# Moving set-up work and the first block's transfers to other engines in a planned recurrence and feed-forward kernel

## The chip, the cores and the metric

The kernel runs on one core of a Trainium2 chip. The metric is the device time of one execution in microseconds; the median of several executions is compared. A profile of one execution gives the rows quoted below; in them PE is TensorE, PEld its weight loads, DVE is VectorE, ACT is ScalarE, POOL is GpSimd and SP is the engine that mostly issues transfers. A name with q (SPq, ACTq) is the engine's own queue of issues and waits.

## What is computed

The reference has three parts, one feeding the next. The first is a recurrence over 768 time steps for 4 x 8 heads of width 40:

```python
for t in range(S):
    y[:, :, t] = einsum('bhd,bhde->bhe', rt, state)
    Sa = einsum('bhde,bhe->bhd', state, at)
    state = state * wt[:, :, None, :] - einsum('bhd,bhe->bhde', Sa, bt)
    state = state + einsum('bhd,bhe->bhde', vt, kt)
...
h = x @ w_in;  x = (h * tanh(softplus(h))) @ w_out
h = x @ w_in2; out = (h * cos(h)) @ w_out2
```

The two feed-forward layers take 3072 tokens of width 320 through 2048 hidden units, in float32, each matmul split into high and low parts that run as fp32r.

## The kernel before

The recurrence is cut into 24 chunks of 32 time steps, and the 32 heads into two halves of 16, so there are 48 steps g = 0 to 47 (chunk c = g // 2, half hf = g % 2). For each step a function pre prepares what does not depend on the state: a load IN, two scans on VectorE (L584, L592), two products AM (L600), a product KB (L606), 32 matmuls (L630), and a masked product (L643) that is stored to DRAM as l_d (L663, L664). For a batch of steps (the first batch has four steps, 0 to 3, the others two) inverse loads l_d back as XM in another layout (L707), runs 28 small steps (L722, L724; on VectorE for the first two batches, on GpSimd from the third), stores t_d (L735) and loads it as TT (L741). halves (L770 to L773) completes the inverse with the masks lowd and lowm, which setup_tf makes (L372 to L380). Then chain runs the part that depends on the state: stages of matmuls rhs (L837), zmm (L851), ztm (L860, L883), rvz (L909), f (L935) and stm (L985), with evictions by ScalarE and VectorE between them. Two steps of a chunk are mates: a stage of one can be held back until the other's is ready, so that both run without a change of TensorE's tile shape.

Every two chunks give the outputs of 256 tokens, a block. yst stores Y of each half to x_d in DRAM (L1004, L1005), and layer1 loads the block back as XR (L1098 to L1100), splits it into XH (L1107) and XL (L1109), runs the first layer's matmuls h_tasks (L1045) and outs (L1026), with Mish on ScalarE (L1123, L1125) and the difference GL on VectorE (L1128). There are 12 such blocks. The second layer (L1060, L1077) follows at the end.

The weights come as pairs of 32-bit words. prep loads each piece (L468), converts it with ScalarE (L475) and two or three VectorE steps (L480, L485), copies the high part (L402 or L404) and has GpSimd subtract it (L515). Its list of pieces, jobs, has 25 for the first layer, 12 of w_in and 13 of w_out. The raw words have three buffers.

All of this is put into the engines' instruction streams by a planner, Plan. Each task has an engine (or a choice), an estimated duration, predecessors, buffers that it takes from rings, and a priority prio where a lower number goes first. run simulates the engines and always takes the task that can begin earliest, then by rank (for TensorE, by tile shape and mates) and prio. The order that results is the order in each engine's stream, and an engine works through its stream strictly in order; the waits in the program follow from the data alone. So predecessors that only the planner knows shape the order and are no waits. The priorities around the change: pre(g) has -5000 + 10g, inverse -5000 + 10(g0 + cnt) - 32, chain(g) -10000 + 10g, the weight words of the first layer -4921, and the first block's input load -9955.

These lines set what the change touches: the order of the weight loads (in prep),

```python
preds=(after if layer == 2 else [tt_ld[2]] if len(loads) >= W1_FREE else [t_in[2]]) + ([t_sw] if late else [])
    + (loads[-AHEAD_W:][:1] * (len(loads) >= AHEAD_W) if len(loads) >= W1_FREE else loads[-1:]),
```

and the short conversion (Prelu with a slope that keeps the sign), which is taken where `two` holds:

```python
two = layer == 1 and not late
```

## Time and profile before

| what | us |
|---|---|
| median of three executions | 1088.33 |
| their lowest and highest | 1087.53, 1093.37 |
| the profiled execution, its own time | 1083.14 |
| its span, first to last instruction | 1081.0 |
| TensorE busy in the span | 1016.0 (94%) |
| VectorE, ScalarE, GpSimd busy | 728.4, 545.7, 419.6 |

The span is what the rows are measured in; the execution's own time holds some 2 us around it. A row of an engine's order of time gives start, duration, engine, line, operation, result and operands with their shapes, how many were merged into the row, and in brackets the idle time of the engine before it with what ended it.

### The profile page before, as it was taken

What the parts mean: (1) busy time and instruction counts of PE and PEld (TensorE: products, weight loads), DVE (VectorE), ACT (ScalarE), POOL (GpSimd) and SP (SyncE); (2) the same over time, 40 slices, a digit from 0 to 9 for tenths busy, and PEclk for the clock granted to TensorE, in tenths of its full rate; (3) what the DMA queues carried; (4) which work ended last, traced back from release to release, by engine and by line L of the source; (5) the groups of instructions that cost most, each with busy time, mean ns of one, the idle gap of its engine ahead of it and who ended that gap; (6) DMA issues with size and microseconds to landing.
All of it is one profiled execution on the core that took longest, in us unless ns stands there. A gap on an engine that the chain in (4) does not pass through costs nothing.

```text
span 1081.0 us, 36651 instructions
## 1 busy us (share of the span) xinstructions
PE 1016.0 (94%) x15112; PEld 934.8 (86%) x15112; DVE 728.4 (67%) x1542; ACT 545.7 (50%) x1338; POOL 419.6 (39%) x862
## 2 busy tenths in 40 slices
PE   3289898999999999999999999999999999999998
PEld 3177787888888988989989999999999999999997
DVE  8598977767857678577653798545555656565555
ACT  1166676664656556566475454444433434353433
POOL 3124665353554627546530144103333333333332
PEclk9999799999999999999999999999999999999999
DMA  4567745646545555456452454211100202010100
GB/s 109 152 196 227 216 130 158 174 114 172 148 124 158 132 151 157 127 136 167 118 144 63 156 164 125 87 47 30 43 13 1 55 1 54 1 40 1 25 1 25
DMA packets 109014, 111.90 MB, mean 104 GB/s; under 512 B 64048, under 2 KB 88624, under 8 KB 108848
## 3 DMA queue, kind: packets, MB, share of 16 engines
q1 hardware_dynamic: 103952, 108.19, 36.2%
q8 instruction: 119, 1.95, 0.8%
q10 hardware_dynamic: 4896, 1.38, 0.6%
q14 instruction: 47, 0.39, 0.1%
HBM read 91.43 MB, written 18.09 MB: 101 GB/s over the span
## 4 chain that ended last, share of the span: by engine, by line
PE 47%; DVE 2%; issue 1%; ACT 0%; DVEq 0%
PE bank L1060 14%; PE bank L1077 13%; PE bank L1045 9%; PE bank L1026 9%; PE bank L1172 1%; PE bank L935 1%; DVE GL L1128 0%; PE bank L883 0%; DVE AU L485 0%; PE bank L837 0%; ACT GH L1125 0%; PE bank L851 0%; PE bank L909 0%; DVE AU L493 0%; DVE FR L919 0%
## 5 line engine op out<-in xcount | busy, mean ns | idle before, releaser
L1211 POOL TENSOR_TENSOR GL<-H,GH 128x512 fp32r<-128x512 f32 x94 | 122.0, 1298 | 239.2 <-ACT GH L1209 223.6
L724 POOL TENSOR_TENSOR XT<-XM 64x14 f32<-64x14 f32 (+6 forms) x294 | 98.4, 335 | 162.9 <-DMA XM<-l_d 129.3
L402 ACT ACTIVATE FL<-bank 64x160 f32<-64x160 f32 (+1 forms) x376 | 101.8, 296 | 117.4 <-PE bank L674 62.5
L1202 ACT ACTIVATE T<-T,half_pi 128x512 f32<-128x512 f32 x96 | 69.4, 723 | 104.3 <-DVE T L1199 104.3
L1128 DVE TENSOR_TENSOR GL<-H,GH 128x512 fp32r<-128x512 f32 x96 | 70.3, 736 | 71.9 <-ACT GH L1125 64.0
L1195 DVE TENSOR_SCALAR T<-bank 128x512 f32<-128x512 f32 x96 | 66.4, 692 | 75.6 <-PE bank L1060 63.4
L722 POOL TENSOR_TENSOR XM<-XM,XT 64x14 f32<-64x14 f32 (+6 forms) x294 | 101.3, 345 | 22.6
L1204 DVE TENSOR_TENSOR H<-bank,T 128x512 f32<-128x512 f32 x96 | 66.1, 689 | 54.4 <-ACT T L1202 53.9
L1123 ACT ACTIVATE H<-bank 128x512 f32<-128x512 f32 x96 | 57.5, 599 | 88.3 <-PE bank L1045 86.1
L1209 ACT ACTIVATE GH<-H 128x512 fp32r<-128x512 f32 x96 | 60.6, 632 | 71.5 <-DVE H L1204 71.5
L1045 PE MATMUL bank<-XH,wih 128*128 128x256 f32 x448 | 94.7, 293 | 0.3 <-ACT XH L1107 0.3
L1045 PE MATMUL bank<-XL,wih 128*128 128x256 f32 x448 | 89.3, 281 | 0.5 <-DVE XL L1109 0.5
L1045 PE MATMUL bank<-XH,wil 128*128 128x256 f32 x448 | 89.3, 281 | 0.0
L1045 PEld LDWEIGHTS bank<-XH,wih 128*128 128x128 f32 x448 | 69.8, 191 | 2.5 <-ACT XH L1107 0.5
L1045 PEld LDWEIGHTS bank<-XL,wih 128*128 128x128 f32 x448 | 69.2, 191 | 0.8 <-DVE XL L1109 0.8
L1045 PEld LDWEIGHTS bank<-XH,wil 128*128 128x128 f32 x448 | 69.1, 191 | 0.0
L1199 DVE SCALAR_TENSOR_TENSOR T<-T,bank 128x512 f32<-128x512 f32 x96 | 65.7, 685 | 2.4
L1045 PE MATMUL bank<-XH,wix 128*128 128x256 f32 x224 | 67.1, 300 | 0.0
L935 PE MATMUL bank<-FR,FL 104*64 104x72 f32 x1536 | 63.2, 240 | 2.4 <-issue 1.1
L1026 PE MATMUL bank<-woh1a,GH 128*128 128x320 f32 x192 | 64.9, 338 | 0.0
L935 PEld LDWEIGHTS bank<-FR,FL 104*64 104x64 f32 x1536 | 56.7, 147 | 7.5 <-DVE FR L919 3.1
L1045 PE MATMUL bank<-XL,wix 128*128 128x256 f32 x224 | 62.9, 281 | 0.0
(189 smaller groups left out, 2859.0 us busy)
## 6 DMA issues: line engine op xcount, KB each, us to landing
VR<-in_vR_dram SPq DMA_DIRECT2D x96, 160.0 KB
IN<-in_inT_dram SPq DMA_DIRECT2D x94, 161.4 KB
FR<-in_rI_dram SPq DMA_DIRECT2D x48, 180.0 KB
FR<-in_vF_dram SPq DMA_DIRECT2D x48, 144.0 KB
RA<-in_w_in_dram SPq DMA_DIRECT2D x12, 512.0 KB
RA<-in_w_out_dram SPq DMA_DIRECT2D x10, 512.0 KB
SV<-in_vS_dram SPq DMA_DIRECT2D x96, 52.0 KB
TMP<-in_w_in_dram SPq DMA_DIRECT2D x8, 512.0 KB
```

The source lines that it names most:

```text
L402: A.activation(o, i, AF.Copy)
L722: IE.tensor_tensor(out=b[:, 0:i, i + 1:16], in0=b[:, 0:i, i + 1:16], in1=tv, op=ALU.add)
L724: IE.tensor_tensor(out=tv, in0=bc(b[:, i:i + 1, i + 1:16], (2 * n, i, w)), in1=bc(b[:, 0:i, i:i + 1], (2 * n, i, w)), op=ALU.mult)
L935: PE.matmul(fp[64 * p:64 * p + 64, qp], fl()[0:104, n * D:n * D + 64], fr()[:, n], start=True, stop=True)
L1026: PE.matmul(o, l[:, f, tsl], r, start=(first and f == 0 and i == 0), stop=(last and f == 1 and i == 2))
L1045: PE.matmul(hp[:, f], pss[i][0], pss[i][1], start=(i == 0), stop=(i == 7))
L1060: PE.matmul(bank[P.at((key, "h"))][:, 0:512], pss[i][0], pss[i][1], start=(i == 0), stop=(i == 7))
L1077: PE.matmul(o, l, r, start=(ft == 0 and i == 0), stop=(ft == NFF - 1 and i == 2))
L1128: gl = P.add(GLE, (dve(512),), lambda eng, Hv=Hv, key=key: EN[eng].tensor_tensor(out=GL_t[P.at((key, "gl"))], in0=Hv(), in1=GH_t[P.at((key ...
L1195: a = P.add("DVE", dve(512), lambda f=f, hv=hv, Tv=Tv: V.tensor_scalar(out=Tv(f), in0=hv(), scalar1=0.25, scalar2=MAGIC, op0=ALU.add, op1= ...
L1202: c = P.add("ACT", act(512, False, 1), lambda f=f, Tv=Tv: A.activation(Tv(f), Tv(f), AF.Sin, scale=-TWO_PI, bias=half_pi), preds=[b], aset ...
L1211: gl = P.add(*((VG, (pool(512), dve(512))) if final and quad == 7 else ("POOL", pool(512))), lambda eng, f=f, Hv=Hv, key=key: EN[eng].tens ...
```

## The change

The diff does eight things. Y's store and the input load of the first block are issued by ScalarE's queue instead of SP's, with an estimated 2.5 us until they land. setup_tf, which makes the masks, runs on GpSimd instead of VectorE. The four clears of SV on VectorE in the first two steps' loads go; setup_v clears these buffers on GpSimd already. The weight loads: the third to the fifth follow the load of XM in the plan (before, the third and fourth followed IN of step 2 and the fifth followed TT's second load), and each of the first five follows the one before it. The weight words' priority goes from -4921 to -4941. Tasks with a priority up to -9890, that is chain and halves of steps 0 to 11, are no longer held back by age or for a mate. The estimate of GpSimd's inverse steps becomes 0.28 us with 0.06 us of latency. The short conversion is limited to the first 30 words.

```diff
--- before.py
+++ after.py
@@ -85,6 +85,7 @@
         "chain.zmm": "32x32", "halves.mm.f": "32x32", "chain.stm": "64x128", "chain.ztm": "full"}
 LEAVE, CHANGE, ENTER = 0.22, 0.12, 0.13
 AGE = 3.0
+EAGER = -1e4 + 110
 WAIT = 8.0
 SP_SAFE = 1.0
 RATE, LAND = 200.0, 1.6
@@ -180,9 +181,9 @@
                             rank = 2.0
                         elif t.mode == last_mode != "full":
                             rank = -1.0
-                        elif t.soft and last_mode == "full" and st - t.ready[e] < AGE:
+                        elif t.soft and t.prio > EAGER and last_mode == "full" and st - t.ready[e] < AGE:
                             rank = 1.5
-                        elif t.mate and last_mode == "full" and st - t.ready[e] < WAIT and t.mate.end is None and (
+                        elif t.mate and t.prio > EAGER and last_mode == "full" and st - t.ready[e] < WAIT and t.mate.end is None and (
                                 t.mate.n_wait or t.mate.ready[e] > st):
                             rank = 1.5
                     key = (max(st - t.pull if e == "DVE" else st, f + SLACK[e]), rank, t.prio + (5e4 if sw else 0), order[id(t)])
@@ -369,15 +370,15 @@
 
     def setup_tf():
 
-        V.memset(lowd, 0.0)
+        G.memset(lowd, 0.0)
         for i in range(4):
             r = slice(32 * i, 32 * i + 32)
-            V.tensor_copy(lowd[r, 16:32], ident[r, 32 * i + 16:32 * i + 32])
+            G.tensor_copy(lowd[r, 16:32], ident[r, 32 * i + 16:32 * i + 32])
         tmp = TB[:, 0]
-        V.tensor_tensor(out=tmp[:, 0:8], in0=lowd[:, 16:24], in1=lowd[:, 24:32], op=ALU.add)
-        V.tensor_tensor(out=tmp[:, 8:12], in0=tmp[:, 0:4], in1=tmp[:, 4:8], op=ALU.add)
-        V.tensor_tensor(out=tmp[:, 12:14], in0=tmp[:, 8:10], in1=tmp[:, 10:12], op=ALU.add)
-        V.tensor_tensor(out=lowm, in0=tmp[:, 12:13], in1=tmp[:, 13:14], op=ALU.add)
+        G.tensor_tensor(out=tmp[:, 0:8], in0=lowd[:, 16:24], in1=lowd[:, 24:32], op=ALU.add)
+        G.tensor_tensor(out=tmp[:, 8:12], in0=tmp[:, 0:4], in1=tmp[:, 4:8], op=ALU.add)
+        G.tensor_tensor(out=tmp[:, 12:14], in0=tmp[:, 8:10], in1=tmp[:, 10:12], op=ALU.add)
+        G.tensor_tensor(out=lowm, in0=tmp[:, 12:13], in1=tmp[:, 13:14], op=ALU.add)
 
     def setup_x():
         G.memset(XM, 0.0)
@@ -423,10 +424,11 @@
     INV_LEAD = 32
     OWN = 2
     SPLIT = 14
-    QUICK = 4
+    QUICK, QUICK_B = 4, 1
     EARLY = 1
+    TWO = 30
     AHEAD_W = 5
-    W1_FREE = 4
+    W1_EARLY, W1_FREE = 2, 5
     DIRECT = 4
     HV_D, HV_P = (0.4, 0.43), 0.52
     B_HI2 = 1.0
@@ -436,7 +438,7 @@
     LOE2, LOD2 = ("POOL", "DVE"), (pool(512), dve(512))
     B_CH, B_HI = 1.3, 0.6
     W1_AFTER = lambda: None
-    W1_G, W1_PRIO = 1, -4921.0
+    W1_G, W1_PRIO = 1, -4941.0
     W2_PRIO = 5e3
     G_POOL = lambda m: m % 2 == 1
 
@@ -466,10 +468,10 @@
                 "p (n w) -> p n w", w=2)
             av = uv = lambda key=key, aring=aring, n=n: STG[aring][P.at((key, "a"))][:, 0:n]
             t0 = P.add("SP", 0.5, lambda raw=raw, src=src: SP.dma_start(raw().rearrange("p n w -> p (n w)"), src),
-                       preds=(after if layer == 2 else [tt_ld[2]] if len(loads) >= W1_FREE else [t_in[2]]) + ([t_sw] if late else []) + (loads[-AHEAD_W:][:1] * (len(loads) >= AHEAD_W) if len(loads) >= W1_FREE else loads[-1:]),
+                       preds=(after if layer == 2 else [tt_ld[2]] if len(loads) >= W1_FREE else [inv_ld[0]] if len(loads) >= W1_EARLY else [t_in[2]]) + ([t_sw] if late else []) + (loads[-AHEAD_W:][:1] * (len(loads) >= AHEAD_W) if len(loads) >= W1_FREE else loads[-1:]),
                        acq=[(rring, (key, "r"))], kb=0.5 * n, prio=prio)
             loads.append(t0)
-            two = layer == 1 and not late
+            two = layer == 1 and not late and len(loads) <= TWO
             f, more = (AF.Prelu, {"alpha": NEGATIVE}) if two else (AF.Copy, {})
             t1 = P.add("ACT", act(n, False),
                        lambda raw=raw, av=av, f=f, more=more: A.activation(
@@ -727,7 +729,7 @@
 
         for i in range(1, 15):
             for add in range(2):
-                t = P.add("POOL" if own else "DVE", 0.1 + 0.0022 * i * (15 - i) if own else 0.165, step(i, add), preds=[t], lat=0.1 if own else 0.04, prio=pr, port=True)
+                t = P.add("POOL" if own else "DVE", 0.28 if own else 0.165, step(i, add), preds=[t], lat=0.06 if own else 0.04, prio=pr, port=True)
         t = P.add("POOL" if own else "DVE", 0.1, lambda: IE.memset(x()[:, 16:512:33], 1.0), preds=[t], prio=pr)
 
         def st():
@@ -797,9 +799,6 @@
             sv = SV_t[P.at(k("SV"))]
             SP.dma_start(sv[64:96, 0], ins["vS"][hf, c, 0])
             SP.dma_start(sv[0:32, 1], ins["vS"][hf, c, 1])
-            if c == 0:
-                V.memset(sv[0:40, 0], 0.0)
-                V.memset(sv[64:104, 1], 0.0)
 
         t3 = P.add("SP", 0.8, f3, preds=[S_V] + held(2), acq=[("SV", k("SV"), 3 if c else 1)], kb=106, prio=pr)
         t1 = P.add("SP", 0.8, f1, preds=[S_V] + held(0), acq=[("FR", k("FR"))], kb=331, prio=pr)
@@ -999,12 +998,14 @@
         if yc == 1:
             xv = x_d[yb].rearrange("(p h e) t -> p e h t", p=2, h=4)[:, :, :, 128 * hf:128 * hf + 128]
 
+            Q = A if yb < QUICK_B else SP
+
             def yst():
                 yv = Y_t[P.at(ykey)].rearrange("r (h b) t -> r h (b t)", b=2)
-                SP.dma_start(xv[0], yv[0:40])
-                SP.dma_start(xv[1], yv[64:104])
-
-            ytask.setdefault(yb, []).append(P.add("SP", 1.0, yst, preds=yevs, rel=[ykey], kb=164, prio=pr if c > 1 else pr - 40))
+                Q.dma_start(xv[0], yv[0:40])
+                Q.dma_start(xv[1], yv[64:104])
+
+            ytask.setdefault(yb, []).append(P.add(dur=1.0, fn=yst, preds=yevs, rel=[ykey], prio=pr if c > 1 else pr - 40, **(dict(eng="ACT", lat=2.5) if yb < QUICK_B else dict(eng="SP", kb=164))))
 
 
     x2st = {}
@@ -1090,16 +1091,17 @@
     def layer1(blk, wready):
         pr0 = blk * 100
         xk = ("x1", blk)
+        Q = A if blk < QUICK_B else SP
         xr = lambda: XR_t[P.at((xk, "xr"))]
         prx = -9.955e3 if blk == 0 else pr0
 
         def ld():
             t = xr()
-            SP.dma_start(t[:, 0:2], x_d[blk][0:256].rearrange("(k p) t -> p k t", p=128))
-            SP.dma_start(t[0:64, 2], x_d[blk][256:320])
-            SP.dma_start(t[64:128, 2], x_d[blk][256:320])
-
-        t = P.add("SP", 1.5, ld, preds=ytask[blk] + [blk_prev[0]], acq=[("XR", (xk, "xr"))], kb=384, prio=prx)
+            Q.dma_start(t[:, 0:2], x_d[blk][0:256].rearrange("(k p) t -> p k t", p=128))
+            Q.dma_start(t[0:64, 2], x_d[blk][256:320])
+            Q.dma_start(t[64:128, 2], x_d[blk][256:320])
+
+        t = P.add(dur=1.4, fn=ld, preds=ytask[blk] + [blk_prev[0]], acq=[("XR", (xk, "xr"))], prio=prx, **(dict(eng="ACT", lat=2.5) if blk < QUICK_B else dict(eng="SP", kb=384)))
         if blk == 0:
             for i, r in enumerate(("PH", "PO", "PH", "PO")):
                 P.add("SP", 0.0, lambda i=i, r=r: P.grow(r, [P.at(("bank", i))], P.time), preds=[t],
@@ -1246,7 +1248,7 @@
     S_G = P.add("POOL", 6.9, setup_g, prio=-1e6)
     S_V = P.add("POOL", 4.5, setup_v, preds=[S_G], prio=-9e5)
     P.ring("TF", 1)
-    S_TF = P.add("DVE", 1.2, setup_tf, preds=[S_G], prio=-4.97e3)
+    S_TF = P.add("POOL", 2.5, setup_tf, preds=[S_G], prio=-4.96e3)
     S_X = P.add("POOL", 1.1, setup_x, prio=-4.97e3)
     state_init = {}
     for g in range(4):
```

## Rows read from the trace of the kernel before

**Rows 1.** Stretches: start:end, length, busy us per engine (xcount), granted clock, DMA share, GB/s.

```profile
0.00:58.00 58.00, 19.21 (x336) 16.68 (x340) 42.64 (x110) 11.71 (x33) 15.70 (x48) 1.00 0.51 141
...
97.60:128.40 30.80, 25.04 (x406) 21.33 (x398) 27.30 (x54) 21.33 (x56) 18.25 (x36) 0.83 0.85 235
115.46:132.10 16.64, 13.44 (x93) 12.64 (x94) 15.62 (x26) 11.65 (x23) 7.98 (x8) 0.71 0.86 233
150.00:191.50 41.50, 36.78 (x917) 32.38 (x915) 32.94 (x84) 28.91 (x81) 22.85 (x68) 0.96 0.60 164
...
577.00:1081.00 504.00, 498.85 (x3473) 469.23 (x3472) 301.38 (x468) 214.90 (x377) 155.39 (x116) 1.00 0.16 47
...
sum 1081.00, PE 1016.02 PEld 934.78 DVE 728.37 ACT 545.71 POOL 419.58; mean PE 84.67 PEld 77.90 DVE 60.70 ACT 45.48 POOL 34.97
```

**Rows 2.** VectorE and GpSimd in order of time, first 31 us.

```profile
7.01 0.71 DVE L592 TENSOR_TENSOR_SCAN RP<-IN,D1R 104x264 f32<-104x264 f32 x1
...
7.63 0.39 DVE L600 TENSOR_TENSOR AM<-IN,PE 40x256 f32<-40x256 f32 x1
...
8.17 3.13 DVE L375 COPY lowd<-ident 32x16 f32<-32x16 f32 x4
...
8.74 1.86 POOL L367 MEMSET VR<- 32x1024 f32 x2
...
12.09 0.42 DVE L600 TENSOR_TENSOR AM<-IN,PE 40x256 f32<-40x256 f32 x1
...
15.05 0.41 DVE L801 MEMSET SV<- 40x416 f32 x1
...
16.00 0.42 DVE L600 TENSOR_TENSOR AM<-RL,PE 40x256 f32<-40x256 f32 x1
...
27.65 1.57 POOL L515 TENSOR_TENSOR wil<-H,wih 128x512 fp32r<-128x512 f32 x1 [15.13 <-DVE wih L404]
...
30.12 0.88 DVE L643 TENSOR_TENSOR AM<-bank,maskG 64x256 f32<-64x256 f32 x2 [2.02 <-PE bank L630]
```

**Rows 3.** Order of time from the last l_d store to TT, queues and VectorE.

```profile
31.03 0.36 ACTq L664 DMA_DIRECT2D l_d<-AM  x1
...
35.87 1.15 ACTq L707 DMA_DIRECT2D XM<-l_d  x2
...
36.71 0.41 SPq L468 DMA_DIRECT2D RL<-in_w_in_dram  x1
...
42.10 0.18 DVE L724 TENSOR_TENSOR XT<-XM 128x14 f32<-128x14 f32 x1 [1.21 <-DMA XM<-l_d]
...
52.27 1.09 ACTq L741 DMA_DIRECT2D TT<-t_d  x2
...
55.96 0.44 DVE L770 STREAM_TRANSPOSE TA<-TT 128x256 f32<-128x256 f32 x1
```

**Rows 4.** Order of time, a GpSimd tensor-tensor and a VectorE scan beside it.

```profile
62.63 1.71 POOL L515 TENSOR_TENSOR wol1a<-H,woh1a 128x512 fp32r<-128x512 f32 x1 [3.59 <-ACT woh1a L402]
...
63.14 1.77 DVE L584 TENSOR_TENSOR_SCAN OB<-IN,D 104x264 f32<-104x264 f32 x1
```

**Rows 5.** The page's groups by line: busy us, mean ns, idle us before, releaser.

```profile
L724 POOL TENSOR_TENSOR XT<-XM 64x14 f32<-64x14 f32 (+6 forms) x294 | 98.4, 335 | 162.9 <-DMA XM<-l_d 129.3
```

**Rows 6.** Order of time from the last Y store of the first block to XH.

```profile
97.24 0.36 SPq L1005 DMA_DIRECT2D x_d<-Y  x1
...
106.08 0.38 SPq L1098 DMA_DIRECT2D XR<-x_d  x1
...
114.57 0.83 ACT L1107 ACTIVATE XH<-XR 128x768 fp32r<-128x768 f32 x1
```

**Rows 7.** TensorE in order of time, one stage alone and two joined.

```profile
107.10 0.69 PE L909 MATMUL bank<-VR 104*64 104x64 f32 x16 [0.29 <-ACT VR L402]
...
151.34 1.15 PE L909 MATMUL bank<-VR 104*64 104x64 f32 x32
```

**Rows 8.** GpSimd in order of time, the last weight word of the first layer.

```profile
190.83 0.73 POOL L515 TENSOR_TENSOR wol1c<-RL,woh1c 128x256 fp32r<-128x256 f32 x1 [4.37 <-ACT woh1c L402]
```

## What I expect, before the run

> **What bounds the kernel now.** I read the busy time of all engines in long stretches first, then the order of time of the first 60 us by engine, then the two places where a transfer is written to DRAM and read back.
>
> The stretches [rows 1] show TensorE working 498.85 of the last 504.00 us. There is nothing to win there unless the work itself changes, and no matmul is added or removed. Of the 1081.0 us span, 65.0 are idle TensorE (1081.00 less the sum of 1016.02), and 38.8 of these lie in the first 58 us: 19.21 busy of 58.00. Another 5.8 lie between 97.60 and 128.40, and 4.7 between 150 and 191.5. In 115.46 to 132.10 the granted clock was 0.71, so part of that stretch ran at the 1.2 GHz level; against 2.4 GHz the 13.44 us of work there lost about 13.44 x 0.29 = 3.9 us. So the end of the kernel is set by how soon TensorE gets steady work: a microsecond of lead at the start is a microsecond at the end, if nothing later takes it back.
>
> What holds the start is one chain. VectorE prepares steps 0 to 3, the last mask product of step 3 goes to DRAM, comes back as XM, is inverted in 28 small VectorE steps, goes to DRAM again and comes back as TT; only then can step 0 proceed. In that first part VectorE hardly pauses [rows 2]: the second AM product of step 0 waits from 8.05 to 12.09 behind the mask set-up, whose four copies take 3.13 us while GpSimd is clearing VR. That is the longest thing in front of the chain that is not part of it.
>
> **The change, part by part.** The mask set-up leaves VectorE. It ran between the two AM products of step 0, from 7.98 (after 7.63 and its 0.39 us) to 12.09: about 4.1 us [rows 2]. The four clears of SV leave too: the first pair costs 16.00 less 15.05 = 0.95 us, the second pair is like it, so 1.9 us. Together 6.0 us. All of it is in front of the last mask product of step 3 at 30.12 and VectorE is busy nearly throughout, so I count all 6.0 as lead. Nothing has to replace the SV clears: setup_v clears both buffers on GpSimd already. On GpSimd the masks cost nine small instructions; the chain does not need them before the halves at 55.96 [rows 3], and GpSimd is idle for the 15.13 us before 27.65 [rows 2]. What they may cost is VectorE's speed: a scan took 1.77 us beside a GpSimd tensor-tensor of 1.71 [rows 4], and 0.71 beside clears [rows 2]. The smallest tensor-tensors that GpSimd does here are the inverse steps, 335 ns each [rows 5]; nine instructions at that price are 3.0 us, and some are smaller. If VectorE stood still for all of it, the lead would be 3.0. Ends 3.0 and 6.0; I take 6.0, since the neighbours in time are clears, beside which the scan kept 0.71.
>
> The page GPSIMD Engine Reference of the Trainium skill, section Key points, says that GpSimd shares its SBUF interfaces with VectorE and contends with VectorE instructions that have two SBUF inputs. The slow scan agrees with it; by that rule the lower end, 3.0, would hold and the sum below would be 6.0 instead of 9.0.
>
> The weight loads are spread. Before, words 3 and 4 are issued from SP right in the flight of XM's read: one at 36.71 beside the read issued at 35.87 [rows 3]. XM arrives at 42.10, 5.1 us after its second issue ended (35.87 + 1.15 = 37.02); TT, as large, comes in 55.96 - 53.36 = 2.6 us. And the write before it took from 31.39 to 35.87, 4.5 us. Without those words both could shrink: the read by up to 2.5, the write by up to 1.6 if it too took 2.9 or so, 4.1 together. Other loads (IN of steps 4 and 5) stay, so the lower end is 0; I take 2.0.
>
> The rank of the words (-4941, ahead of steps 6 and 7's preparation instead of behind) moves VectorE work that has to be done before the first block ends in any case. Its upper bound is the 4.7 us of idle TensorE in 150 to 191.5, its lower one is the slower rival below; I take 0. The limit TWO = 30 changes nothing at all: the first layer has 25 loads, so every word that took the short conversion still does. The longer estimate of GpSimd's inverse steps (0.28 + 0.06 us) only makes the planner agree better with the measured 335 ns [rows 5]: 0.
>
> The first block's Y store and input load move to ScalarE's queue. Now the second Y store ends at 97.60, but the load of XR is issued at 106.08 because SP has other loads in front of it, and XH starts at 114.57 [rows 6]. On ScalarE the load waits only for the write of Y: at most the 4.5 us seen for l_d. So 8.5 us of waiting shrink by 4.0 to 8.5; I take 6 us earlier input. What that is worth is not 6: TensorE has chain work meanwhile and the pool is the 5.8 us of idle and the 3.9 us of clock, 9.7 in all [rows 1]. Ends 0 and 9.7; I take half of the 6, 3.0, because the work brought forward is missing later. What it costs: seven issues (four of Y, three of XR, at the 0.38 us of the first of XR) on ScalarE, 2.7 us, and a wait in its stream. Behind that wait stand the evictions RS, VR, FR of steps 4 and 5, and TensorE's next stage behind them. ScalarE is busy 21.33 of 30.80 us there, and the planner puts other work into the 2.5 us that it expects. Ends 0 and -4.5 (one whole write); I take -1.0. SP's order loses seven issues and gains none.
>
> The page DMA: Bandwidth & Descriptors of the Trainium skill, section Issuing engines are not separate DMA queues, says that issuing from several engines saves only the sequencer's time, which is usually small. By it this part would save its seven issues of 0.38 us, a lead of 2.7 and a worth of 1.3, and the sum would be 7.3. The row disagrees: between 97.60 and 106.08 the place in SP's order is what costs.
>
> EAGER: steps 0 to 11 no longer wait for a mate or for age between dense stretches. A joint stage of 32 matmuls took 1.15 us where 16 took 0.69 [rows 7]: 0.23 saved per join. Six mated stages, four pairs from step 4 to 11: at most 5.5 us lost. What an earlier step can win is the 4.7 us idle in 150 to 191.5. Ends -5.5 and +4.7; I take -1.0, nearer to the middle.
>
> Sum: 6.0 + 2.0 + 3.0 - 1.0 - 1.0 = 9.0 us faster, from 1083.14 (1081.0 of span and 2.1 around it) to 1074.1. That execution lies 5.2 below the median shown, 1088.33; against the median the forecast is 1079.3. All times below are on the median's scale.
>
> **The rivals.** More than that: the XM transfers become as quick as TT's (4.1), and the early input recovers the whole idle and clock pool (9.7): 6.0 + 4.1 + 9.7 - 2.0 = 17.8, so 1070.5. For it: the clock fell exactly as the first block began with gaps around it. Against: that block is also held by Mish and GL, not by its input alone. 0.22.
>
> The lead is given back: the last weight words are done on GpSimd at 191.5 [rows 8], and the first block's last products need them. If the words do not come sooner, block 0 ends at the same time, TensorE idles in front of it, and only some 2 us of filler remain: 1086.3. For it: the last five words wait for earlier buffers. Against: they follow TT's load, which comes earlier. 0.18.
>
> Slower: words 3 to 5 now stand one behind the other and behind XM's load in SP's order, with step 4 to 6's IN loads around them. A place late in SP's order cost XR's load 8.5 us [rows 6]. If the third word gets such a place, all later words, which reuse its three buffers, come 8.5 us later, and the last one ends at 200 instead of 191.5. TensorE can fill some 2.5 us with chain work: 6 us slower, 1094.3. It decides once the last GpSimd word ends later than 191.5 and TensorE's idle time in 150 to 200 exceeds the 4.7 of now by more than the lead won earlier. For it: VectorE and the queue are full in that stretch. Against: words 3 and 4 went at 36.71 and later already, and XM should now be read before that. 0.14.
>
> That the change does not do what it says is true of TWO alone, and costs nothing.
>
> **How the numbers follow.** The forecast, 5.4 to 13 us faster, has 0.46, with its own range 1075 to 1083. A measurement can tell about 0.5%, 5.4 us. Faster is 0.46 + 0.22 = 0.68, same 0.18, slower 0.14. The range goes from 1067 (21 us: the larger case and most of the 4.7 us that the rank could win) to 1090, which leaves out most of the slower case and little else.
>
> **What would show it.** In the changed trace VectorE's second AM product of step 0 should start near 8.1, not 12.1, and step 3's last mask product near 24; XM should land near 34 and TT near 48. XR's load should be on ScalarE's queue within 5 us of the Y store, and the first wih matmul near 101. TensorE's idle time before 58 should fall from 38.8 to about 31, and later stretches should not grow. I am wrong if VectorE's scans stretch beside the masks on GpSimd, if ScalarE stands more than 4 us at XR's load, if the last GpSimd word is not earlier than 191.5, or if TensorE's idle time moves from the first 58 us to 150 to 200.

## The result: slower by half a per cent

The changed kernel took 1095.36 us, the kernel before 1088.89 us (medians of 20 runs each); the ratio is 1.0054, 95% interval 1.0036 to 1.0073. The forecast was 1079.3. The profiled execution took 1089.47 us, its span is 1087.8 (1083.14 and 1081.0 before).

The stretches of the changed kernel, in the columns of [rows 1]:

```profile
0.00:58.00 58.00, 23.75 (x523) 20.64 (x523) 42.85 (x107) 17.25 (x47) 23.07 (x58) 1.00 0.61 172
58.00:97.60 39.60, 32.14 (x880) 28.52 (x881) 30.93 (x90) 20.46 (x61) 8.54 (x6) 1.00 0.51 140
97.60:128.40 30.80, 21.89 (x341) 19.73 (x332) 21.45 (x47) 15.36 (x44) 12.80 (x32) 0.77 0.78 222
128.40:150.00 21.60, 12.84 (x175) 11.74 (x176) 19.10 (x35) 12.11 (x24) 7.83 (x9) 0.53 0.58 157
150.00:191.50 41.50, 40.72 (x901) 36.75 (x901) 30.24 (x76) 29.54 (x83) 29.25 (x81) 1.00 0.50 135
...
577.00:1081.00 504.00, 502.24 (x3869) 471.92 (x3866) 301.93 (x481) 221.31 (x403) 167.85 (x129) 1.00 0.17 50
```

The same view of the kernel before, the two stretches that [rows 1] leave out:

```profile
58.00:97.60 39.60, 35.74 (x1027) 31.88 (x1016) 36.24 (x102) 24.85 (x74) 8.19 (x6) 1.00 0.66 195
...
128.40:150.00 21.60, 21.58 (x396) 20.37 (x397) 15.12 (x30) 14.40 (x34) 16.55 (x35) 0.92 0.46 123
```

Read the first number behind the length, TensorE's busy time. The start won 23.75 - 19.21 = 4.5 us. Then 3.6 were lost up to 97.6, 3.2 up to 128.4, 8.7 up to 150, and 3.9 won after it: by 191.5 TensorE has been busy 7.0 us less (131.34 against 138.35), and the span is 6.8 longer. In the whole span it is busy for 1016.9 us (1016.0 before), so 5.9 of the 6.8 us are idle time. Between 128.4 and 150 the clock was granted at 0.53, nearly the 1.2 GHz level, in a stretch where TensorE was busy for 12.84 of 21.60 us. So the loss lies between 58 and 150.

The start went nearly as forecast. VectorE and GpSimd of the changed kernel in order of time, answering to [rows 2, 3]:

```profile
7.59 0.82 DVE L602 TENSOR_TENSOR AM<-IN,PE 40x256 f32<-40x256 f32 x2
...
11.73 2.31 POOL L376 COPY lowd<-ident 32x16 f32<-32x16 f32 x4
...
11.91 0.88 DVE L645 TENSOR_TENSOR AM<-bank,maskG 64x256 f32<-64x256 f32 x2 [0.53 <-PE bank L632]
...
24.69 0.88 DVE L645 TENSOR_TENSOR AM<-bank,maskG 64x256 f32<-64x256 f32 x2 [2.06 <-PE bank L632]
...
31.91 1.15 ACTq L709 DMA_DIRECT2D XM<-l_d  x2
...
36.04 0.17 DVE L726 TENSOR_TENSOR XT<-XM 128x14 f32<-128x14 f32 x1 [2.38 <-DMA XM<-l_d]
...
50.89 0.45 DVE L772 STREAM_TRANSPOSE TA<-TT 128x256 f32<-128x256 f32 x1
```

The two AM products run together, the masks are made on GpSimd without VectorE slowing (a pair of mask products takes 0.88 us, as before), and the first inverse starts 6.1 us earlier (42.10 to 36.04). The answer to [rows 6]:

```profile
91.10 0.47 ACTq L1006 DMA_DIRECT2D x_d<-Y  x1
...
94.67 0.41 ACTq L1100 DMA_DIRECT2D XR<-x_d  x1
...
102.25 0.84 ACT L1109 ACTIVATE XH<-XR 128x768 fp32r<-128x768 f32 x1
...
138.95 1.28 ACT L1125 ACT_TABLE_LOAD   x1
```

The kernel before, ScalarE:

```profile
121.92 1.28 ACT L1123 ACT_TABLE_LOAD   x1
```

The input load goes out 3.1 us behind the issue of the Y store (91.57) instead of 8.5, XH comes 12.3 us earlier than before, and yet ScalarE's table for the first Mish is loaded 36.7 us behind XH (7.4 before, at 121.92). The last weight word on GpSimd, answering to [rows 8]:

```profile
188.13 0.73 POOL L517 TENSOR_TENSOR wol1c<-RL,woh1c 128x256 fp32r<-128x256 f32 x1 [0.39 <-ACT woh1c L403]
```

It comes 2.7 us earlier than before (190.83).

### The profile page after: what moved, and what is told of

Its sections match the earlier page's. It is cut to its first block, busy times and chain, and to the rows that moved or that the text cites. A ratio compares the mean times of both kernels' runs of the same rounds, so it can differ in the third digit from the quotient of the medians.

```text
span 1087.8 us, 36624 instructions
## 1 busy us (share of the span) xinstructions
PE 1016.9 (93%) x15112; PEld 937.4 (86%) x15112; DVE 721.2 (66%) x1528; ACT 543.9 (50%) x1337; POOL 444.8 (41%) x871
## 4 chain that ended last, share of the span: by engine, by line
PE 74%; DVE 11%; DMA 6%; issue 4%; POOL 2%; ACT 2%; SPq 1%; ACTq 0%; DVEq 0%; POOLq 0%
PE bank L1046 15%; PE bank L1027 14%; PE bank L1061 14%; PE bank L1078 13%; PE bank L934 3%; PE bank L908 2%; PE bank L635 2%; PE bank L882 2%; PE bank L850 2%; PE bank L676 1%; PE bank L769 1%; DVE SV L945 1%; PE bank L767 1%; PE bank L836 1%; PE bank L632 1%
## 5 line engine op out<-in xcount | busy, mean ns | idle before, releaser
L726 POOL TENSOR_TENSOR XT<-XM 64x14 f32<-64x14 f32 (+6 forms) x294 | 103.2, 351 | 181.0 <-DMA XM<-l_d 160.1
L403 ACT ACTIVATE FL<-bank 40x160 f32<-40x160 f32 (+1 forms) x376 | 101.5, 295 | 112.9 <-PE bank L676 52.8
L1130 DVE TENSOR_TENSOR GL<-H,GH 128x512 fp32r<-128x512 f32 x96 | 73.2, 768 | 76.2 <-ACT GH L1127 68.6
L724 POOL TENSOR_TENSOR XM<-XM,XT 64x14 f32<-64x14 f32 (+6 forms) x294 | 106.9, 364 | 22.6
L918 DVE TENSOR_TENSOR FR<-bank,maskR 64x256 f32<-64x256 f32 x96 | 38.9, 419 | 40.5 <-PE bank L908 26.6
```

Of the source, the lines that this page charges most:

```text
L403: A.activation(o, i, AF.Copy)
L724: IE.tensor_tensor(out=b[:, 0:i, i + 1:16], in0=b[:, 0:i, i + 1:16], in1=tv, op=ALU.add)
L726: IE.tensor_tensor(out=tv, in0=bc(b[:, i:i + 1, i + 1:16], (2 * n, i, w)), in1=bc(b[:, 0:i, i:i + 1], (2 * n, i, w)), op=ALU.mult)
L1130: gl = P.add(GLE, (dve(512),), lambda eng, Hv=Hv, key=key: EN[eng].tensor_tensor(out=GL_t[P.at((key, "gl"))], in0=Hv(), in1=GH_t[P.at((key ...
```

## The experiments

The versions were measured in four sets. Each time is a median, and each ratio is that to the kernel before in the same set (its medians there: 1087.01 for e1 to e4, 1086.71 for e5 to e8, 1087.64 for e9 to e12, 1086.51 for e13 to e16), with a 95% interval. The ratio can differ a little from the quotient of the two medians (0.9961 for e1, with a ratio of 0.9984). What follows goes by the ratios.

| run | what it is | us | ratio |
|---|---|---|---|
| e1 | change without the ScalarE-queue part | 1082.82 | 0.9984 (0.9957 to 1.0010) |
| e2 | before with the ScalarE-queue part alone | 1098.86 | 1.0130 (1.0096 to 1.0164) |
| e3 | change without EAGER | 1097.64 | 1.0115 (1.0079 to 1.0151) |
| e4 | before with the masks and clears alone | 1085.20 | 0.9999 (0.9970 to 1.0027) |
| e5 | change, its plan kept, transfers issued by SP | 1084.41 | 0.9983 (0.9955 to 1.0010) |
| e6 | e1, its plan kept, transfers issued by ScalarE | 1092.71 | 1.0054 (1.0028 to 1.0079) |
| e7 | change with an earlier Mish | 1095.39 | 1.0077 (1.0044 to 1.0109) |
| e8 | e1 with an earlier Mish | 1090.15 | 1.0042 (1.0011 to 1.0073) |
| e9 | change, Y stores by SP | 1087.14 | 0.9995 (0.9970 to 1.0020) |
| e10 | change, XR load by SP | 1090.45 | 1.0025 (1.0000 to 1.0050) |
| e11 | change, first Y store later in the program | 1087.25 | 1.0005 (0.9982 to 1.0027) |
| e12 | before with the weight words alone | 1096.65 | 1.0079 (1.0051 to 1.0108) |
| e13 | e1 without the weight words | 1084.95 | 0.9991 (0.9968 to 1.0015) |
| e14 | e1 with the words' old rank | 1094.38 | 1.0086 (1.0050 to 1.0122) |
| e15 | e1 with the words' old load order | 1090.19 | 1.0038 (1.0013 to 1.0063) |
| e16 | e5 without the weight words | 1084.49 | 0.9999 (0.9968 to 1.0029) |

### First: which part costs it

e1, e2, e3 and e4:

```diff
-    QUICK, QUICK_B = 4, 1        # e1: in the changed kernel
+    QUICK, QUICK_B = 4, 0
+    QUICK, QUICK_B = 4, 1        # e2: in the kernel before, with the lines on Q
-EAGER = -1e4 + 110               # e3: in the changed kernel
+EAGER = -1e9
+        G.memset(lowd, 0.0)      # e4: in the kernel before, setup_tf on GpSimd
-            if c == 0:           #     and no clears of SV on VectorE
```

> The whole change, but Y's store and XR's load of the first block stay on SP's queue. Theory 1 (the ScalarE queue costs it: the first block's input comes early, but in ScalarE's order its first Mish then stands 27 rows behind XH instead of 9, and SP waits for Y's writes): 1080 to 1085 us against 1088.9 before and 1095.4 with the whole change; the first Mish within 10 us of XH, TensorE idle under 6 us in 97 to 150. Rival 1 (EAGER: stages no longer joined): still 1093 to 1097. Rival 2 (weight words placed and ranked differently): still 1093 to 1097.

> The kernel before with Y's store and XR's load of the first block on ScalarE's queue, nothing else. Theory 1: 1095 to 1103 us (the loss without the 6 us lead of the masks), the first Mish some 40 rows behind XH in ScalarE's order and over 25 us later. Rivals 1 and 2: 1086 to 1090, no loss.

> The whole change with EAGER out of reach, so that steps 0 to 11 are held back for age and mates as before. Theory 1: 1093 to 1098 us, no gain. Rival 1: 1080 to 1087.

> The kernel before with the masks made on GpSimd and without the four SV clears on VectorE. Theory 1: the 6 us lead (XM read lands near 36 instead of 42) reaches the end: 1081 to 1085 us. Rival 3 (a lead at the start is always taken back by the weight words, done at 191): 1087 to 1090.

The ScalarE-queue part carries the whole loss: without it the ratio is 0.9984, alone it costs 1.3%. EAGER does not make the loss; without it the change is if anything slower. Masks and clears alone keep their lead up to the first inverse (XT at 36.50) and have none at the input: XR's load goes out at 105.85, 106.08 before, and the time is the same. The queue part is also not what makes the input early. In e1, which issues it from SP, XR's load goes out at 94.43 us (94.67 in the changed kernel); in e2, which has the queue part alone, at 106.19:

```profile
94.43 0.42 SPq L1100 DMA_DIRECT2D XR<-x_d  x1
```

### Second: the plan's order or the queue

The planner writes out every engine's order from its own estimates, so moving two transfers changes the order of everything behind them. In the changed kernel the first Mish is ScalarE's 50th instruction behind XH, in the kernel before the 12th (the expectations count merged rows, 27 and 9); that order was my first theory. e5 and e6 part it from the queue: the planner gets the same tasks as in the changed kernel (or in e1), and only the function that issues the transfer uses the other queue. In the compiled programs TensorE, VectorE, GpSimd and ScalarE then have the same instructions in the same order as in the kernel compared with, but for the transfers. e7 and e8 take the planner's surcharge for a table change off the first block's Mish.

```diff
-            Q = A if yb < QUICK_B else SP      # e5 (the task stays eng="ACT")
+            Q = SP
-            Q = A if yb < QUICK_B else SP      # e6, QUICK_B = 0 (eng="SP" stays)
+            Q = A if yb < 1 else SP
-t.prio + (5e4 if sw else 0)                    # e7, e8
+t.prio + (5e4 if sw and not (t.aset == ("mish",) and t.prio < -9e3) else 0)
```

> The changed kernel with its plan untouched, so that TensorE, VectorE, GpSimd and ScalarE get the same instructions in the same order as in the changed kernel; only the two Y stores and the XR load of block 0 are issued by SP, at the place in SP's order where the plan had them on ScalarE. Theory 1a (what costs is the order that the planner makes, with ScalarE's first Mish behind 27 other rows): the loss stays, 1091 to 1097, first Mish again over 30 us behind XH. Theory 1b (what costs is the queue: ScalarE held at the transfers, or transfers that hold each other's completion counters): the loss goes, 1081 to 1086, and the first Mish comes earlier by the 6 us or more. XR load expected 1 to 5 us behind the Y store in both.

> The mirror image: the plan of the variant without the ScalarE-queue part (1082.8 there), whose compute engines keep their order, but the Y stores and the XR load of block 0 are issued by ScalarE at their planned places. Theory 1a (order costs): near 1083, 1080 to 1086, first Mish within 10 us of XH. Theory 1b (queue costs): 1088 to 1097, with ScalarE standing 3 us or more at the XR load, and everything behind it late.

> The changed kernel, with the planner's surcharge for a change of ScalarE's table not applied to the Mish of block 0, so that it is placed 21 rows behind XH and not 27. Theory 1a: part of the loss comes back: first Mish some 8 us earlier relative to XH, 1086 to 1092. Theory 1b: no change, 1093 to 1097. If the extra table loads cost more than the order gives (each 1.3 us): over 1097.

> Without the ScalarE-queue part and without the surcharge on Mish in block 0: the second and later Mish of that block come as soon as their product is done, instead of at 138.7 us. Theory 1a (ScalarE's order at the start of the dense layers is what decides): 1076 to 1081, faster than the variant with the surcharge (1082.8). Rival: the chain of the scan sets the pace there and the early Mish only delays its evictions: 1083 to 1090.

The order theory fell. e5 has the changed kernel's order, with its late Mish (table at 132.9), and is 0.7% faster than it by the ratios; e6 has e1's order and is slower than e1 by 0.7%. An earlier Mish in the plan gained nothing in e7 (its table is loaded 30.1 us behind XH instead of 36.7) and lost in e8. What costs is the queue. SP's queue in order of time, changed kernel:

```profile
74.89 0.77 SPq L737 DMA_DIRECT2D t_d<-XM  x2
81.65 0.29 SPq L795 DMA_DIRECT2D VR<-in_vR_dram  x1
...
82.59 0.35 SPq L470 DMA_DIRECT2D TMP<-in_w_out_dram  x1
```

The same instructions in e5:

```profile
76.00 0.77 SPq L737 DMA_DIRECT2D t_d<-XM  x2
76.87 0.54 SPq L795 DMA_DIRECT2D VR<-in_vR_dram  x1
...
78.63 0.35 SPq L470 DMA_DIRECT2D TMP<-in_w_out_dram  x1
```

In the changed kernel SP stands for 6.0 us (75.66 to 81.65) in front of a load that has no data in common with Y. The waits of SP's queue between 70 and 100 us (instruction <- what released it: us in total, times, longest) say what it waited for, changed kernel:

```profile
SPq L795 <- DMA x_d<-Y: 5.9, 1, 5.9
...
SPq L470 <- DMA x_d<-Y: 2.5, 1, 2.5
```

In e5 SP waits for the landing of Y only 0.3 us, at XR's load, which reads that data; e6 has the wait of 5.9 us again. The compiled program gives the reason. It lists, for each transfer, the counters that it waits on (DMAHW0 to DMAHW7; the numbers count each engine's own transfers):

```
changed kernel, SP       57 FR load    waits DMAHW6 ...
                         58 SV load    waits DMAHW1 ...
                         63 t_d store  waits DMAHW6
                         64 VR load    waits DMAHW7, PE, Activation
changed kernel, ScalarE  15 Y store    waits DMAHW7, DVE
                         16 Y store    waits DMAHW0
```

In this program the transfers take eight completion counters in turn, over both queues together, and each waits for the one that held its counter before. The Y store took counter 7 between SP's transfers 57 and 58; eight transfers later the turn comes to the VR load. On one queue such a wait is short, as the eighth transfer back was issued before (in e5 the longest in this stretch is 1.7 us, an SV load behind a weight load). With two queues that drift apart, SP waits for a store that ScalarE can issue only once VectorE has made Y, and that then has to land. VectorE and ScalarE's queue, changed kernel:

```profile
79.40 0.27 DVE L953 TENSOR_TENSOR Y<-bank,PE 104x128 f32<-104x128 f32 x1
...
79.71 0.53 ACTq L1005 DMA_DIRECT2D x_d<-Y  x1
```

In e5 the store stands behind the VR load in SP's order (76.87 and 80.79), and in SP's queue nothing but the input load waits for it.

### Third: counters, or ScalarE held at the input load

Both transfers are on ScalarE in the changed kernel, and ScalarE also stood 2.89 us at XR's load. e9 leaves only XR there, e10 only Y. e11 keeps both on ScalarE but writes the first Y store into the program six SP tasks later, so that the VR load takes over another counter; on ScalarE the store then stands behind the evictions FR, FL and RS. The orders of the four computing engines are in all three those of the changed kernel.

```diff
-            Q = A if yb < QUICK_B else SP      # e9
+            Q = SP
-        Q = A if blk < QUICK_B else SP         # e10
+        Q = SP
-                Q.dma_start(xv[0], yv[0:40])   # e11; "later" calls it
-                Q.dma_start(xv[1], yv[64:104]) # six SP tasks later, once
+                P.later(lambda: (Q.dma_start(xv[0], yv[0:40]),
+                Q.dma_start(xv[1], yv[64:104])))
```

> Plan and compute order of the changed kernel; the Y stores are issued by SP, only the XR load of block 0 stays on ScalarE's queue. Theory 2a (the loss comes through the completion counters, which both queues take in turn: a load of SP has to wait until the Y store eight transfers before it has landed): SP's VR load, at 81.65 in the changed kernel, goes out near 77 as it did with all three on SP, and the time is near 1084 to 1087. Theory 2b (ScalarE itself, held 2.9 us at the XR load, makes the loss): 1090 to 1096, with VR out at 77 all the same.

> The complement: Y stores on ScalarE's queue, XR load on SP, plan and compute order of the changed kernel. Theory 2a: the wait of 5.9 us at SP's VR load for the Y store is there again, VR goes out at 81 to 82, and most of the loss stays: 1090 to 1095. Theory 2b: ScalarE is not held at the XR load, 1084 to 1087.

> The changed kernel with both transfers on ScalarE's queue, but the first Y store is written into the program six of SP's tasks later (on ScalarE behind one more cast of a weight word), so that SP's VR load is no longer the transfer that takes over its counter; plan and compute order else the same. Theory 2a: VR goes out near 77 and not at 81.65, the weight words and ScalarE's casts behind it come 3 to 5 us earlier, and a good part of the loss comes back: 1085 to 1091. Theory 2b, or any theory in which ScalarE's queue is slower by itself: 1093 to 1097.

SP's and ScalarE's queues and ScalarE in order of time, e11:

```profile
75.23 0.77 SPq L737 DMA_DIRECT2D t_d<-XM  x2
...
76.11 0.62 SPq L795 DMA_DIRECT2D VR<-in_vR_dram  x1
...
78.14 0.35 SPq L470 DMA_DIRECT2D TMP<-in_w_out_dram  x1
...
82.54 0.53 ACTq L1005 DMA_DIRECT2D x_d<-Y  x1
...
82.70 0.62 ACT L403 ACTIVATE wix<-H 128x512 fp32r<-128x512 f32 x1
...
83.22 0.66 ACT L477 ACTIVATE H<-TMP 128x512 f32<-128x512 f32 x1
...
91.19 0.41 ACTq L1100 DMA_DIRECT2D XR<-x_d  x1
```

The changed kernel's H of that word, and what ScalarE did before it:

```profile
80.62 1.25 ACT L403 ACTIVATE FR<-bank 32x160 f32<-32x160 f32 x4 [1.59 <-DVE SV L945]
...
83.36 0.62 ACT L403 ACTIVATE wix<-H 128x512 fp32r<-128x512 f32 x1
87.91 0.66 ACT L477 ACTIVATE H<-TMP 128x512 f32<-128x512 f32 x1 [3.93 <-DMA TMP<-in_w_out_dram]
```

In e11 the first Y store goes out 2.8 us later (82.54 against 79.71), yet the VR load goes out 5.5 us earlier, the weight word's conversion 4.7, even the input load 3.5, and the time is that of the kernel before (1.0005). e11 keeps later waits of this kind:

```profile
SPq L579 <- DMA XR<-x_d: 4.3, 1, 4.3
SPq L470 <- DMA x_d<-Y: 3.6, 1, 3.6
```

Added up from each run's view of SP's waits between 60 and 150 us, in us (SP's own load of XR, which reads Y, left out):

| run | longest wait for Y | all for Y | all for XR | ratio |
|---|---|---|---|---|
| e2 | 9.0, an IN load | 15.3 | 2.8 | 1.0130 |
| e3 | 5.9, the VR load | 9.2 | 4.5 | 1.0115 |
| e7 | 5.9, the VR load | 8.9 | 4.6 | 1.0077 |
| changed kernel | 5.9, the VR load | 8.6 | 4.6 | 1.0054 |
| e6 | 5.9, the VR load | 9.4 | 4.6 | 1.0054 |
| e10 | 5.9, the VR load | 7.7 | 0.4 | 1.0025 |
| e11 | 3.6, a weight load | 4.5 | 4.5 | 1.0005 |
| e9 | none | 0 | 3.5 | 0.9995 |
| e5 | none | 0 | 1.0 | 0.9983 |

So the VR load's wait for Y goes with the loss, and XR's wait does not part the changed kernel from e11. e10 keeps the Y store on ScalarE and the wait of 5.9 us; in its profile TensorE has been busy 131.2 us by 191.5, as in the changed kernel (131.3), against 136.6 in e9. Its ratio of 1.0025 lies between the two, and its interval overlaps both, so whether XR's part adds anything is not shown. In e9 ScalarE idles 3.9 us at XR's load, longer than in the changed kernel, and e9 shows no cost of it.

One thing goes away together with the counter's wait in e9 and e11. In the changed kernel ScalarE idles 1.6 us at the first Y store, until VectorE has made Y, and FR starts at 80.62 (79.40 in e11). By wix, behind FR, FL and RS, 0.7 us of this is left (83.36 against 82.70), while H of the word behind the VR load is 4.7 us late. The rows thus put most of the loss on the counter; no run takes away one without the other.

### Fourth: why the rest is worth nothing

With the queue undone e1 gains only 0.2%, within its interval, though its lead at the start is there (XT at 37.07). e12 to e16 ask the weight words.

```diff
-    W1_FREE = 4                                # e12, in the kernel before
-    W1_G, W1_PRIO = 1, -4921.0
+    W1_EARLY, W1_FREE = 2, 5
+    W1_G, W1_PRIO = 1, -4941.0
+    W1_EARLY, W1_FREE = 4, 4                   # e13, e15, e16
+    W1_G, W1_PRIO = 1, -4921.0                 # e13, e14, e16
```

> The kernel before with the weight words alone changed: two more loads let go behind the inverse's loads, the free-running loads from the fifth on, rank -4941. My forecast had these at nothing: 1085 to 1089. Rival from the forecast (words placed late in SP's order): over 1092, with the first words' casts later. If the words are what paces the first dense layer: under 1084, with the last GpSimd word before 185 us (190.8 before).

> Without the ScalarE-queue part and without the weight words' part: masks on GpSimd, buffers cleared there alone, the limit on postponing small tiles, and the new cost of the own inverse's steps. Theory 3a (the words' part is what gives back the lead of 6 us at the first inverse): 1078 to 1082, faster than the kernel before and than the variant with the words (1082.8). Theory 3b (the lead is lost at the XR load's place in SP's order, whatever the words do): 1083 to 1088, XR load again near 105.

> Without the ScalarE-queue part, words' loads let go as changed but at the old rank -4921. If the rank is what puts the words ahead of the scan and makes the hole between 128 and 150 us (15.59 busy with it, 21.58 before): the hole is gone, over 19 busy there. If the loads' order makes it: hole stays, under 17. Time 1080 to 1087 by either.

> The complement: words' rank -4941, their loads let go as before. If the rank makes the hole between 128 and 150 us: under 17 busy there, 1084 to 1092. If the loads' order makes it: over 19 busy, 1080 to 1086.

> The plan of the change without the words' part, with the Y stores and the XR load issued by SP at the places that the plan gave them on ScalarE. If an early XR load (near 95) and the lead at the first inverse can be kept together once neither the counters nor the words stand against them: 1075 to 1082, the fastest so far. If the dense layers then only start on words that are not there yet: 1083 to 1090, with the hole behind the first group of h products.

The words' part alone costs the kernel before 0.8%. Their profiled execution (span 1102.4, above its median) shows where, in the columns of [rows 1]:

```profile
128.40:150.00 21.60, 9.08 (x115) 8.32 (x116) 16.19 (x25) 8.76 (x20) 12.70 (x22) 0.73 0.34 88
150.00:191.50 41.50, 39.08 (x807) 36.10 (x806) 25.89 (x64) 22.10 (x65) 29.21 (x84) 0.89 0.47 134
```

They are done earlier (the last GpSimd word starts at 186.7, 190.83 before), but TensorE works 9.08 us between 128.4 and 150 instead of 21.58. Beside the other parts, in one profile each, rank alone (e15) leaves 14.21 there, load order alone (e14) 12.21, neither (e13) 17.86: there either half leaves a deeper hole than neither. My expectation that one of them would be clean was wrong, and so was e14's time (1094.38, where I had 1080 to 1087). e1, with both, leaves 15.59, and its hole can be read in ScalarE's order of time:

```profile
117.77 0.94 ACT L403 ACTIVATE woh1b<-H 128x512 fp32r<-128x512 f32 x2 [1.13 <-DVE H L487]
...
130.22 0.99 ACT L403 ACTIVATE FL<-bank 64x160 f32<-64x160 f32 x4 [5.21 <-PE bank L676]
131.11 0.65 ACT L477 ACTIVATE H<-RL 128x512 f32<-128x512 f32 x1
133.68 0.63 ACT L403 ACTIVATE wih<-H 128x512 fp32r<-128x512 f32 x1 [1.92 <-DVE H L487]
...
138.69 1.28 ACT L1125 ACT_TABLE_LOAD   x1
```

The next words were issued by 118.97; ScalarE converts them from 131.11 on, because three evictions FL that wait for the scan's products (9.5 us of idle) stand before them, and the next products of the dense layer start at 141.13, 20 us behind the last at 121.2. But taking the words' part out does not bring the lead back: e13 has 0.9991 where e1, with it, has 0.9984, and e16 0.9999 where e5 has 0.9983. In e13 the input is loaded at 104.0, late again in SP's order. e16, which has neither the counters nor the words against it, loads the input at 99.3 and comes out equal too (its profiled execution, 1095.16 us, lies far above its median of 1084.49). No version was faster than the kernel before by more than its interval; the nearest are e1 and e5, whose intervals end at 1.0010. So where the lead goes has been read in single profiles, at a different place in each, and is not shown by a run. Nor was it settled why rank and load order together cost less (e1) than either does without the other (e14, e15); each edit makes the planner choose a new order.

## Why the prediction was wrong

Two steps failed. The forecast was 9.0 us faster and 5.9 us slower came (0.54%), a miss of 15. About 10 of it are the ScalarE-queue part (2.0 faster forecast, 0.7% or 7.6 us slower from e1 to the result), about 5 the worth of the lead (7.0 faster forecast for the rest, 0.2% or 1.7 us measured in e1).

- **Y and XR on ScalarE's queue, +3.0 less 1.0:** the main step that failed, with the wrong sign. I wrote that SP's order loses seven issues and gains none. It gained waits: 5.9 and 2.5 us for Y, because the transfers of both queues share the program's eight counters. The part alone cost 1.3%, and within the change 0.7% (e1 against the result). Its direct aims were met in the changed kernel (input 3.1 us behind Y; ScalarE 2.89 us at the load, under my limit of 4), but e1 has the input as early without it. The price was on the queue that I took to be relieved. With the same plan the version issued by SP (e5) is 0.7% faster than the changed kernel, so the move gained nothing over SP. As a gain of such a move the Trainium skill's DMA: Bandwidth & Descriptors, section Issuing engines are not separate DMA queues, names only the sequencer's issue time. The runs here show no gain at all.
- **A lead at the start is a lead at the end:** this premise gave the 6.0 and the 2.0 their worth. The lead was there (next two points), but e4, which has the masks and clears alone, measured 0.9999, and no version kept more than 0.2%.
- **Masks and clears, 6.0:** about right in size where I read it. The last mask product came 5.4 us earlier (30.12 to 24.69), the second AM product at about 8.0 (the row of the kernel before gives 7.63 + 0.39 = 8.02 where the prediction has 8.05). VectorE did not slow: its scans took 0.69 to 0.75 us beside the masks, so the lower end of 3.0 does not hold here. The Trainium skill's GPSIMD Engine Reference, section Key points, speaks of contention between GpSimd and VectorE instructions that have two SBUF inputs. In these traces a GpSimd operation paid for it (last section).
- **XM's transfers, 2.0:** XT's lead is 6.1 us of which 5.4 were there at the mask product; the transfers gave 0.6. TA came 5.1 us earlier, at 50.89. TensorE's idle time before 58 fell from 38.8 to 34.3, not to 31.
- **Weight words, 0:** wrong for the words' part alone, where e12 measured +0.8%; beside the other parts it makes no difference (e1 against e13). The rival for slower had the right part of the change for e12 and the wrong sign test: the last word started earlier (186.7 in e12, 188.1 in the changed kernel, 190.83 before), not later, and the hole opened at 128 to 150, not behind 150. That this rival named 6 us and 6 came is luck, as the loss has another cause.
- **EAGER, -1.0:** e3, without it, is slower still (1.0115 against 1.0054), so it does not cost what I took.
- **The rival "lead given back", 0.18:** the lead was given back in e4 and e13, but not through the last words. In both XR's load is late in SP's order; e16, with an earlier load, came out equal too, so that this is the reason is not shown.
- **Signs that I named:** XM's first use came at 36.04 and TT's at 50.89, not near 34 and 48; the first wih product came at 104.66, not 101; "later stretches should not grow" failed between 58 and 150, which the signs of being wrong did not name.

## What to carry to other kernels

Before moving a transfer to another queue, look up in the compiled program which transfer takes over its completion counter. If that one is on the other queue and due earlier, it will wait for a store that it has nothing to do with; here writing the moved store later in the program undid this. A lead at the start is worth what the next hand-overs pass on: here 5 to 6 us at the first inverse were worth nothing measurable at the end in any version, with the input early (e1, e5) or late (e4, e13) and with the weight words changed or not.

## What the runs showed of the hardware

A transfer waited 5.9 us for an unrelated one of the other queue, in five kernels (the changed one, e3, e6, e7, e10) to the tenth, and 9.0 us in e2. The wait is made by the program's eight shared counters and not by a queue's bandwidth: e11 moved the same bytes over the same queues without it, and with 4.5 us of waits for Y in place of 8.6.

GpSimd's four copies of 32x16 took 2.31 us in the changed kernel, where VectorE's took 3.13 before; VectorE beside them kept its times. But in e4 and seven other versions the same four copies took 0.88 us, and a sum of 128x4 that takes 0.20 us in the changed kernel took 1.48. GpSimd and VectorE in order of time, e4:

```profile
11.47 0.88 POOL L376 COPY lowd<-ident 32x16 f32<-32x16 f32 x4
...
12.71 1.48 POOL L379 TENSOR_TENSOR TB<-TB 128x4 f32<-128x4 f32 x1
...
12.86 0.69 DVE L586 TENSOR_TENSOR_SCAN PE<-IN,D 104x264 f32<-104x264 f32 x1
13.47 0.66 DVE L608 TENSOR_TENSOR KB<-RL,RP 104x512 f32<-104x512 f32 x1
```

The long sum ends at 14.19, 0.06 us behind VectorE's KB product (14.13); in the changed kernel the long copies end at 14.04, 0.05 behind KB (13.99). So whichever small GpSimd operation meets the scan and the product is stretched until they are over, while they keep their length. In [rows 4] it was the VectorE scan that was long. What decides who waits, no run here shows.
